# GpSimd's copies tied to points in VectorE's list, in a linear-attention kernel for one core

## Chip, cores, metric

One core of a Trainium2 chip. The time is device microseconds of one execution, the median over several; lower is better. The traced span of an execution is 1.8 us shorter than its time (kernel before: span 177.8, time 179.6), so spans are compared with spans and times with times. "Changed" is the kernel after the change. The engines' short names: PE is TensorE, DVE is VectorE, ACT is ScalarE, POOL is GpSimd, SP is SyncE (here it only issues the transfers). SBUF is the on-chip memory that all tiles but the matmul results are in; PSUM holds those. A run is called slow when it is over 1.5% above the fastest run of the same kernel in the same rounds, else fast.

## The reference, cut

```python
# B, H, S, D = 1, 32, 2048, 128, bf16
phi_q = jnp.where(q > 0, q + 1, jnp.exp(q)) + 1e-6
phi_k = jnp.where(k > 0, k + 1, jnp.exp(k)) + 1e-6
kv  = einsum("bhsd,bhse->bhde", phi_k, v)
z   = einsum("bhsd->bhd", phi_k)
num = einsum("bhqd,bhde->bhqe", phi_q, kv)
den = einsum("bhqd,bhd->bhq", phi_q, z)[..., None] + 1e-6
return num / den
```

The kernel uses phi(x) = (min(exp(x), 1) + eps) + max(x, 0) and keeps the two terms apart, as two matmuls into one PSUM tile. A head has 16 tiles of 128 rows.

## The kernel before, the parts concerned

Every piece of work has a name and stands in a fixed list for its engine; a list is run in order, and each piece waits for the pieces that it names.

```python
NI, NO, NE, NR, NV, NQ, NK = 7, 12, 2, 2, 2, 2, 2     # buffers: inputs, outputs, em, rk, v1, ...
WARM = (60, 30)                                        # dummy matmuls at the start, in batches
def kv_parts(h): return WHOLE
def gate(name, h): return []                           # no extra waits
# --- cut ---
# em: min(exp(k),1)+eps; all 16 tiles, in SBUF, DVE
add("DVE", f"em{h}.{i}", ... tensor_scalar(em_sb, em_sb, 1.0, EPS, op0=ALU.min, op1=ALU.add) ...)
# relu(k): tiles 0-7 on DVE, tiles 8-15 on GpSimd
add("DVE", f"rkd{h}.{i}", ... tensor_scalar(rk_sb, k_sb, 0.0, None, op0=ALU.max) ...)
add("POOL", f"rkp{h}.{i}", ... tensor_scalar(rk_sb, k_sb, BIG, 0.0, op0=ALU.min, op1=ALU.max),
    over("ldk", ...) + freed(NR, h, ("kv", kv_parts)) + gate("rkp", h))
# v beside its column of ones, on GpSimd
add("POOL", f"v1{h}.{i}", ... tensor_copy(v1_sb, v_sb) ...,
    [f"ldv{h}.{i}"] + freed(NV, h, ("kv", kv_parts)) + gate("v1", h))
# kv{h}: 32 matmuls; T{h}: 16 transposes of q; n{h}.0 / n{h}.1: 12 and 4 tiles of num and den
# r{h}.0: reciprocal of 12 den (PSUM); f{h}.0: num * that, 12 tiles (PSUM to SBUF); r.1, f.1: 4 tiles
# emq{h}: as em, for q; rqb{h}: relu of 8 transposed q tiles, read from PSUM
```

One steady stretch of the DVE list: `r9.1 rqb11 f9.1 r10.0 f10.0 emq11.0 em13.0 rkd13.0`. The SyncE list holds all loads and stores; it has `... st18.0 st25.0 ldv30.0 ldk31.0 ...` near its end.

## Time and profile before

| | before |
|---|---|
| median time | 177.51 us (177.2 to 177.63, 3 runs) |
| traced span | 177.8 us |
| busy: PE, DVE, ACT, POOL | 161.9, 158.4, 154.4, 71.5 us |
| DMA bytes | 67.12 MB |

The busy times are summed over the span. Three of the four are within 24 us of the span, and the transfers are busy for 95.1% of it, so the question is in which stretches, and for what, one engine waits for another. Two lines of the groups of instructions on GpSimd say when its work starts today. Columns: line, engine, operation, shape and count; busy us, mean ns; idle before it and what ended that.

```profile
L318 POOL TENSOR_SCALAR la<-la 128x1024 bf16<-128x1024 bf16 x32 | 36.1, 1137 | 44.1 <-PE la L329 33.5 <-DMA la<-in_k_dram 10.6
L322 POOL COPY la<-la 128x1024 int32<-128x1024 int32 (+1 forms) x33 | 35.3, 1076 | 44.0 <-PE la L329 22.4 <-DMA la<-in_v_dram 21.7
```

L329 is the kv product. GpSimd is idle until a kv product frees a buffer, or a load lands, and then starts at once: nothing relates its starts to DVE.

### The profile page before, as it was taken

To read this page: it belongs to the slowest core of one execution; us is meant where nothing else is said; L and a number is where in the kernel's file an instruction comes from. 1 tells how busy PE (TensorE), PEld (TensorE's weight loads), DVE (VectorE), ACT (ScalarE), POOL (GpSimd) and SP (SyncE) were. 2 spreads that over 40 slices of the span, in tenths; PEclk is the share of its full clock that TensorE was granted. 3 is DMA by queue.
4 is the path that set the end of the run, shared out by engine and by line. 5 is a ranking of instruction groups with operands and counts; after the bars stand their busy time and mean duration, and the time that the engine had idled before them with its cause. 6 is when DMAs were issued, how large, how long until landed. Compare 5 with 4: busy or idle time off the path is not lost.

```text
span 177.8 us, 6416 instructions
## 1 busy us (share of the span) xinstructions
PE 161.9 (91%) x2842; PEld 158.1 (89%) x2842; DVE 158.4 (89%) x266; ACT 154.4 (87%) x131; POOL 71.5 (40%) x71
## 2 busy tenths in 40 slices
PE   2986999999999999999889999988999989999870
PEld 1976999999999999999789999978999889989770
DVE  0156899999999999998999999999999999989973
ACT  2599799999999999999898999978999979994600
POOL 1253818417454246262723626264256424360000
PEclk9999999999999999999999999999999999999968
DMA  5999999999999999999999999999999945999973
GB/s 171 323 407 416 411 404 406 412 404 410 408 406 409 406 417 411 407 411 417 412 417 414 420 414 416 416 414 417 412 405 418 414 196 183 285 417 412 418 313 120
DMA packets 19179, 67.52 MB, mean 380 GB/s; under 512 B 2128, under 2 KB 2512, under 8 KB 19152
## 3 DMA queue, kind: packets, MB, share of 16 engines
q1 hardware_dynamic: 19152, 67.12, 95.1%
q8 instruction: 22, 0.36, 0.8%
q14 instruction: 5, 0.04, 0.1%
HBM read 50.33 MB, written 16.78 MB: 377 GB/s over the span
## 4 chain that ended last, share of the span: by engine, by line
PE 43%; DVE 20%; DMA 18%; issue 5%; SPq 4%; ACT 4%; POOL 3%; DVEq 0%; POOLq 0%
PE la L329 17%; DMA la<-in_k_dram 11%; PE la L364 9%; PE la L366 8%; PE la L340 8%; DVE la L380 8%; DMA out_dram<-la 7%; SPq L296 4%; DVE la L314 4%; DVE la L311 3%; DVE la L352 2%; ACT la L343 2%; DVE la L345 2%; POOL la L318 2%; POOL la L322 2%
## 5 line engine op out<-in xcount | busy, mean ns | idle before, releaser
L380 DVE TENSOR_TENSOR la<-la 128x1536 bf16<-128x1536 f32 (+2 forms) x65 | 77.7, 1199 | 2.0 <-DMA out_dram<-la 1.4
L366 PE MATMUL la<-la 128*128 128x129 bf16 x512 | 69.2, 222 | 0.0
L364 PE MATMUL la<-la 128*128 128x129 bf16 x512 | 69.1, 221 | 0.0
L329 PE MATMUL la<-la 128*128 128x129 bf16 x1024 | 64.0, 219 | 2.0 <-ACT la L349 1.4
L343 ACT ACTIVATE la<-la 128x2048 bf16<-128x2048 bf16 (+1 forms) x33 | 60.1, 1825 | 6.5 <-PE la L366 6.0
L308 ACT ACTIVATE la<-la 128x2048 bf16<-128x2048 bf16 (+1 forms) x33 | 61.3, 1860 | 2.1 <-DMA la<-in_k_dram 1.9
L329 PEld LDWEIGHTS la<-la 128*128 128x128 bf16 x1024 | 59.9, 97 | 2.7 <-DVE la L278 1.5
L318 POOL TENSOR_SCALAR la<-la 128x1024 bf16<-128x1024 bf16 x32 | 36.1, 1137 | 44.1 <-PE la L329 33.5
L322 POOL COPY la<-la 128x1024 int32<-128x1024 int32 (+1 forms) x33 | 35.3, 1076 | 44.0 <-PE la L329 22.4
L366 PEld LDWEIGHTS la<-la 128*128 128x128 bf16 x512 | 50.0, 98 | 0.0
L364 PEld LDWEIGHTS la<-la 128*128 128x128 bf16 x512 | 47.8, 98 | 0.0
L340 PE MATMUL la<-la 128*128 128x128 bf16 x512 | 34.8, 222 | 7.0 <-DMA la<-in_q_dram 3.6
L340 PEld LDWEIGHTS la<-la 128*128 128x128 bf16 x512 | 29.6, 99 | 9.0 <-issue 4.0
L359 PE MATMUL la<-la 128*128 128x3 bf16 (+1 forms) x192 | 32.6, 170 | 2.5 <-DVE la L380 2.5
L349 ACT ACTIVATE la<-la 128x1024 bf16<-128x1024 bf16 x32 | 32.6, 1019 | 2.5 <-PE la L340 2.5
L311 DVE TENSOR_SCALAR la<-la 128x2048 bf16<-128x2048 bf16 (+1 forms) x33 | 23.3, 706 | 3.1 <-ACT la L308 3.1
L314 DVE TENSOR_SCALAR la<-la 128x1024 bf16<-128x1024 bf16 x32 | 18.0, 566 | 7.4 <-DMA la<-in_k_dram 7.3
L345 DVE TENSOR_SCALAR la<-la 128x2048 bf16<-128x2048 bf16 (+1 forms) x33 | 22.3, 677 | 0.4 <-ACT la L343 0.4
L359 PEld LDWEIGHTS la<-la 128*128 128x128 bf16 x192 | 18.9, 99 | 3.5 <-DVE la L380 3.1
L352 DVE TENSOR_SCALAR la<-la 128x1024 bf16<-128x1024 bf16 x32 | 21.3, 667 | 0.7 <-ACT la L343 0.7
L373 DVE RECIPROCAL la<-la 128x12 f32<-128x12 f32 (+2 forms) x65 | 12.8, 198 | 2.2 <-PE la L366 1.4
L334 ACT ACTIVATE la<-la 128x129 bf16<-128x129 f32 x32 | 9.0, 281 | 1.0 <-PE la L329 1.0
(14 smaller groups left out, 13.5 us busy)
## 6 DMA issues: line engine op xcount, KB each, us to landing
la<-in_k_dram SPq DMA_DIRECT2D x31, 512.0 KB, 13.9
la<-in_q_dram SPq DMA_DIRECT2D x31, 512.0 KB, 13.9
la<-in_v_dram SPq DMA_DIRECT2D x31, 512.0 KB, 13.3
out_dram<-la SPq DMA_DIRECT2D x31, 512.0 KB, 13.2
la<-in_q_dram SPq DMA_DIRECT2D x2, 256.0 KB, 3.0
la<-in_k_dram SPq DMA_DIRECT2D x2, 256.0 KB, 5.2
la<-in_v_dram SPq DMA_DIRECT2D x2, 256.0 KB, 7.6
out_dram<-la SPq DMA_DIRECT2D x2, 192.0 KB, 2.1
```

The source lines that it names most:

```text
L308: add("ACT", f"ek{h}.{i}", lambda e, a=a, b=b: e.activation(em_sb[:, h % NE, a:b], k_sb[:, h % NI, a:b], ACT.Exp), [f"ldk{h}.{i}"] + freed ...
L311: add("DVE", f"em{h}.{i}", lambda e, a=a, b=b: e.tensor_scalar(em_sb[:, h % NE, a:b], em_sb[:, h % NE, a:b], 1.0, EPS, op0=ALU.min, op1=AL ...
L318: add("POOL", f"rkp{h}.{i}", lambda e, a=a, b=b: e.tensor_scalar(rk_sb[:, h % NR, a:b], k_sb[:, h % NI, a:b], BIG, 0.0, op0=ALU.min, op1=A ...
L322: add("POOL", f"v1{h}.{i}", lambda e, a=a, b=b: e.tensor_copy(v1_sb[:, h % NV, a:b, 0:D].bitcast(i32), v_sb[:, h % NI, a:b].bitcast(i32)), ...
L329: ins = e.matmul(kv_ps, lhsT=src[:, j], rhs=v1_sb[:, h % NV, j, 0:NC], start=(j + part == 0), stop=(j == NT - 1 and part == 1))
L340: ins = e.transpose(xT[:, j], q_sb[:, h % NI, j], ident[:])
L343: add("ACT", f"eq{h}.{i}", lambda e, a=a, b=b: e.activation(emq_sb[:, h % NQ, a:b], xT[:, a:b], ACT.Exp), [f"T{h}.{i}"] + freed(NQ, h, ("n ...
L349: add("ACT", f"rqa{h}", lambda e: e.activation(rq_sb[:, h % NQ, 0:n], xT[:, 0:n], ACT.Relu), over("T", h, q_parts, 0, n) + freed(NQ, h, (" ...
L359: e.matmul(_ap(o_ps[:, :], o + D, [[NC, m]]), lhsT=ones[:], rhs=epsr[:, 0:m], start=True, stop=False, skip_group_check=True)
L364: e.matmul(to, lhsT=emq_sb[:, h % NQ, t], rhs=kvs_sb[:, h % NK], start=False, stop=False, skip_group_check=True)
L366: ins = e.matmul(to, lhsT=rq_sb[:, h % NQ, t], rhs=kvs_sb[:, h % NK], start=False, stop=True, skip_group_check=True)
L380: return e.tensor_tensor(out=_ap(o_sb[:, :, :, :], first(o_sb[:, h % NO, t0, 0:1]) - first(o_sb[:, :, :, :]), [[m * D, nb], [D, m], [1, D] ...
```

## The change

The intent: put GpSimd's two pieces of a head beside DVE work that doesn't need the SBUF ports which the two engines share (the prediction names the page and the trace lines for this), and order everything else around that. The diff, cut to its core:

```diff
-WARM = (60, 30)
+WARM = (60, 15, 15)
 def kv_parts(h):
-    return WHOLE
+    return HALVES
 def gate(name, h):
-    return []
+    if h < 3:
+        return []
+    return [f"r{h - 3}.0"] if name == "v1" else [f"f{h - 3}.0"]
 # the five lists are written anew; two excerpts:
 # DVE, around head 10
-  r9.1 rqb11 f9.1 r10.0 f10.0 emq11.0 em13.0 rkd13.0 r10.1 rqb12 f10.1
+  r9.1 rqb11 f9.1 emq11.0 r10.0 rkd13.0 f10.0 em13.0 rqb12 r10.1 f10.1
 # SP, the end
-  ldk30.0 st17.0 ldv29.0 ldq29.0 st18.0 st25.0 ldv30.0 ldk31.0 st16.0 ldv31.0 st21.0 ldq31.0 st23.0 ...
+  ldv29.0 ldq29.0 ldq30.0 st15.0 ldv30.0 ldv31.0 ldk31.0 ldq31.0 st16.0 st17.0 st18.0 ...
```

More of the change, by code (lines that the diff above doesn't have):

```diff
@@ L54, in gate @@
 def gate(name, h):
-    return []
+    if h < 3:
+        return []
+    return [f"r{h - 3}.0"] if name == "v1" else [f"f{h - 3}.0"]
 ORDER = {
     "PE": """
-        T0.0 T0.1 w1 w0 T1.0 kv0.0 kv1.0 n0.0 n0.1 T2.0 kv2.0 n1.0 T3.0 n1.1 kv3.0 n2.0 T4.0 n2.1 kv4.0 n3.0 T5.0
-        n3.1 kv5.0 n4.0 T6.0 n4.1 kv6.0 n5.0 n5.1 T7.0 kv7.0 n6.0 T8.0 n6.1 kv8.0 n7.0 T9.0 n7.1 kv9.0 n8.0 T10.0
-        n8.1 kv10.0 n9.0 T11.0 n9.1 kv11.0 n10.0 T12.0 n10.1 kv12.0 n11.0 T13.0 n11.1 kv13.0 n12.0 T14.0 n12.1
-        kv14.0 n13.0 T15.0 n13.1 kv15.0 n14.0 T16.0 n14.1 kv16.0 n15.0 T17.0 n15.1 kv17.0 n16.0 n16.1 T18.0 kv18.0
-        n17.0 T19.0 n17.1 kv19.0 n18.0 T20.0 n18.1 kv20.0 n19.0 T21.0 n19.1 kv21.0 n20.0 T22.0 n20.1 kv22.0 n21.0
-        T23.0 n21.1 kv23.0 n22.0 T24.0 n22.1 kv24.0 n23.0 n23.1 T25.0 kv25.0 n24.0 T26.0 n24.1 kv26.0 n25.0 T27.0
-        n25.1 kv27.0 n26.0 T28.0 n26.1 kv28.0 n27.0 T29.0 n27.1 kv29.0 n28.0 T30.0 n28.1 kv30.0 n29.0 T31.0 n29.1
-        kv31.0 n30.0 n30.1 n31.1 n31.0 n31.2
+        w2 T0.1 T0.0 w1 w0 T1.0 kv0.0 kv0.1 n0.0 kv1.0 kv1.1 T2.0 n0.1 n1.0 kv2.0 kv2.1 T3.0 n1.1 kv3.0 kv3.1 n2.0
+        T4.0 n2.1 kv4.0 kv4.1 n3.0 T5.0 n3.1 kv5.0 kv5.1 n4.0 T6.0 n4.1 kv6.0 kv6.1 n5.0 T7.0 n5.1 kv7.0 kv7.1 n6.0
+        T8.0 n6.1 kv8.0 kv8.1 n7.0 T9.0 n7.1 kv9.0 kv9.1 n8.0 T10.0 n8.1 kv10.0 kv10.1 n9.0 T11.0 n9.1 kv11.0 kv11.1
+        n10.0 T12.0 n10.1 kv12.0 kv12.1 n11.0 T13.0 n11.1 kv13.0 kv13.1 n12.0 T14.0 n12.1 kv14.0 kv14.1 n13.0 T15.0
+        n13.1 kv15.0 kv15.1 n14.0 T16.0 n14.1 kv16.0 kv16.1 n15.0 T17.0 n15.1 kv17.0 kv17.1 n16.0 T18.0 n16.1 kv18.0
+        kv18.1 n17.0 T19.0 n17.1 kv19.0 kv19.1 n18.0 T20.0 n18.1 kv20.0 kv20.1 n19.0 T21.0 n19.1 kv21.0 kv21.1 n20.0
+        T22.0 n20.1 kv22.0 kv22.1 n21.0 T23.0 n21.1 kv23.0 kv23.1 n22.0 T24.0 n22.1 kv24.0 kv24.1 n23.0 T25.0 n23.1
+        kv25.0 kv25.1 n24.0 T26.0 n24.1 kv26.0 kv26.1 n25.0 T27.0 n25.1 kv27.0 kv27.1 n26.0 T28.0 n26.1 kv28.0
+        kv28.1 n27.0 T29.0 n27.1 kv29.0 kv29.1 n28.0 T30.0 n28.1 kv30.0 kv30.1 n29.0 T31.0 n29.1 kv31.0 kv31.1 n30.0
+        n30.1 n31.0 n31.1 n31.2
@@ L68 @@
     """,
     "DVE": """
-        v1ones0 rkd0.0 em0.1 rkd1.0 rqb0 em0.0 eps0 em1.0 emq0.1 emq0.0 rqb1 v1ones1 eps1 rkd2.0 eps2 ones emq1.0
-        rkd3.0 em2.0 r0.0 f0.0 em3.0 rqb2 r0.1 rkd4.0 f0.1 r1.0 emq2.0 f1.0 em4.0 rkd5.0 r1.1 rqb3 f1.1 r2.0 f2.0
-        emq3.0 em5.0 rkd6.0 rqb4 r2.1 f2.1 r3.0 emq4.0 f3.0 em6.0 r3.1 rqb5 rkd7.0 f3.1 r4.0 emq5.0 f4.0 em7.0 r4.1
-        f4.1 rqb6 r5.0 f5.0 emq6.0 rkd8.0 em8.0 r5.1 rqb7 f5.1 r6.0 emq7.0 f6.0 rkd9.0 em9.0 r6.1 rqb8 f6.1 r7.0
-        emq8.0 f7.0 rkd10.0 em10.0 r7.1 rqb9 f7.1 r8.0 emq9.0 f8.0 rkd11.0 em11.0 r8.1 rqb10 f8.1 r9.0 rkd12.0 f9.0
@@ L75 @@
-        emq10.0 em12.0 r9.1 rqb11 f9.1 r10.0 f10.0 emq11.0 em13.0 rkd13.0 r10.1 rqb12 f10.1 rkd14.0 r11.0 emq12.0
-        f11.0 em14.0 r11.1 rqb13 f11.1 r12.0 f12.0 emq13.0 rkd15.0 em15.0 r12.1 rqb14 f12.1 rkd16.0 r13.0 emq14.0
-        f13.0 em16.0 r13.1 rqb15 f13.1 r14.0 f14.0 emq15.0 em17.0 rkd17.0 r14.1 rqb16 f14.1 r15.0 rkd18.0 f15.0
-        emq16.0 em18.0 r15.1 f15.1 rqb17 r16.0 f16.0 emq17.0 em19.0 rkd19.0 r16.1 rqb18 f16.1 r17.0 emq18.0 f17.0
-        rkd20.0 em20.0 r17.1 rqb19 f17.1 r18.0 f18.0 emq19.0 rkd21.0 em21.0 r18.1 rqb20 f18.1 r19.0 emq20.0 f19.0
@@ L80 @@
-        em22.0 rkd23.0 rkd22.0 rqb21 r19.1 r20.0 f19.1 f20.0 emq21.0 em23.0 rkd24.0 rqb22 r20.1 f20.1 r21.0 emq22.0
-        f21.0 em24.0 rqb23 r21.1 f21.1 r22.0 emq23.0 rkd25.0 f22.0 em25.0 r22.1 f22.1 rqb24 r23.0 f23.0 emq24.0
-        rkd26.0 em26.0 r23.1 rqb25 f23.1 r24.0 emq25.0 f24.0 em27.0 rkd27.0 r24.1 rqb26 f24.1 r25.0 emq26.0 f25.0
-        rkd28.0 em28.0 r25.1 rqb27 f25.1 r26.0 emq27.0 f26.0 rkd29.0 em29.0 r26.1 rqb28 f26.1 r27.0 emq28.0 f27.0
-        rkd30.0 em30.0 r27.1 rqb29 f27.1 r28.0 f28.0 emq29.0 rkd31.0 em31.0 rqb30 r28.1 f28.1 r29.0 emq30.0 f29.0
@@ L85 @@
-        emq31.0 r29.1 rqb31 r30.0 f29.1 f30.0 r30.1 f30.1 r31.1 f31.1 r31.0 r31.2 f31.0 f31.2
+        rkd0.0 ones v1ones0 emq0.1 rqb0 emq0.0 rkd1.0 em0.0 em0.1 v1ones1 eps0 eps1 em1.0 eps2 emq1.0 rqb1 r0.0 f0.0
+        rkd3.0 rkd2.0 em2.0 em3.0 rqb2 emq2.0 r0.1 f0.1 r1.0 rkd4.0 f1.0 em4.0 rqb3 r1.1 rkd5.0 f1.1 r2.0 emq3.0
+        f2.0 em5.0 rqb4 r2.1 rkd6.0 f2.1 r3.0 emq4.0 f3.0 em6.0 rqb5 r3.1 rkd7.0 f3.1 r4.0 emq5.0 f4.0 em7.0 rqb6
+        r4.1 f4.1 r5.0 emq6.0 f5.0 em8.0 rqb7 r5.1 f5.1 rkd8.0 r6.0 emq7.0 f6.0 em9.0 rqb8 r6.1 f6.1 rkd10.0 rkd9.0
@@ new lines @@
+        r7.0 emq8.0 f7.0 rkd11.0 rqb9 r7.1 em10.0 f7.1 r8.0 emq9.0 f8.0 em11.0 rqb10 r8.1 f8.1 rkd12.0 r9.0 emq10.0
+        f9.0 em12.0 r9.1 rqb11 f9.1 emq11.0 r10.0 rkd13.0 f10.0 em13.0 rqb12 r10.1 f10.1 rkd14.0 r11.0 emq12.0 f11.0
+        em14.0 r11.1 rqb13 f11.1 rkd15.0 r12.0 emq13.0 f12.0 em15.0 r12.1 rqb14 f12.1 rkd16.0 r13.0 emq14.0 f13.0
+        em16.0 r13.1 rqb15 f13.1 rkd17.0 r14.0 emq15.0 f14.0 em17.0 r14.1 rqb16 f14.1 rkd18.0 r15.0 emq16.0 f15.0
+        em18.0 rqb17 r15.1 rkd19.0 f15.1 r16.0 emq17.0 f16.0 em19.0 rqb18 r16.1 rkd20.0 f16.1 r17.0 emq18.0 f17.0
@@ new lines @@
+        em20.0 rqb19 r17.1 rkd21.0 f17.1 r18.0 emq19.0 f18.0 em21.0 rqb20 r18.1 f18.1 rkd22.0 r19.0 emq20.0 f19.0
+        em22.0 rqb21 r19.1 f19.1 rkd23.0 r20.0 emq21.0 f20.0 em23.0 rqb22 r20.1 rkd24.0 f20.1 r21.0 emq22.0 f21.0
+        em24.0 r21.1 rqb23 f21.1 emq23.0 r22.0 rkd25.0 f22.0 em25.0 rqb24 r22.1 f22.1 rkd26.0 emq24.0 r23.0 f23.0
+        em26.0 r23.1 rqb25 f23.1 emq25.0 r24.0 rkd27.0 f24.0 em27.0 rqb26 r24.1 f24.1 emq26.0 r25.0 f25.0 em28.0
+        rqb27 r25.1 f25.1 rkd29.0 r26.0 rkd28.0 f26.0 emq27.0 rqb28 em29.0 r26.1 f26.1 r27.0 rkd30.0 f27.0 emq28.0
@@ L86 @@
+        rqb29 r27.1 emq29.0 f27.1 r28.0 em30.0 f28.0 em31.0 rqb30 r28.1 f28.1 r29.0 rkd31.0 f29.0 emq30.0 emq31.0
+        rqb31 r29.1 r30.0 f29.1 f30.0 r30.1 f30.1 r31.0 f31.0 r31.1 f31.1 r31.2 f31.2
     """,
     "ACT": """
-        rqa0 ek0.1 ek0.0 eq0.1 eq0.0 ek1.0 eq1.0 kvs0 rqa1 ek2.0 kvs1 ek3.0 eq2.0 kvs2 rqa2 ek4.0 eq3.0 kvs3 rqa3
+        eq0.1 eq0.0 rqa0 ek0.0 ek1.0 ek0.1 eq1.0 kvs0 rqa1 ek2.0 kvs1 ek3.0 eq2.0 rqa2 kvs2 ek4.0 eq3.0 kvs3 rqa3
         ek5.0 eq4.0 kvs4 rqa4 ek6.0 eq5.0 kvs5 rqa5 ek7.0 eq6.0 kvs6 rqa6 ek8.0 eq7.0 kvs7 rqa7 ek9.0 eq8.0 kvs8
@@ L92 @@
         ek18.0 eq17.0 kvs17 rqa17 ek19.0 eq18.0 kvs18 rqa18 ek20.0 eq19.0 kvs19 rqa19 ek21.0 eq20.0 kvs20 rqa20
-        ek22.0 eq21.0 rqa21 kvs21 ek23.0 eq22.0 kvs22 rqa22 ek24.0 eq23.0 kvs23 rqa23 ek25.0 eq24.0 kvs24 rqa24
-        ek26.0 eq25.0 kvs25 rqa25 ek27.0 eq26.0 kvs26 rqa26 ek28.0 eq27.0 kvs27 rqa27 ek29.0 eq28.0 kvs28 rqa28
-        ek30.0 eq29.0 kvs29 rqa29 ek31.0 eq30.0 kvs30 rqa30 eq31.0 kvs31 rqa31
+        ek22.0 eq21.0 kvs21 rqa21 ek23.0 eq22.0 kvs22 rqa22 ek24.0 eq23.0 kvs23 rqa23 ek25.0 eq24.0 kvs24 rqa24
@@ L96 @@
+        ek26.0 eq25.0 kvs25 rqa25 ek27.0 eq26.0 kvs26 rqa26 ek28.0 eq27.0 kvs27 rqa27 ek29.0 eq28.0 rqa28 kvs28
+        ek30.0 eq29.0 kvs29 rqa29 ek31.0 eq30.0 kvs30 rqa30 eq31.0 rqa31 kvs31
     """,
     "POOL": """
-        ident0 ident rkp0.0 rkp1.0 v10.1 v10.0 v11.0 v12.0 rkp2.0 rkp3.0 v13.0 v14.0 rkp5.0 rkp4.0 v15.0 rkp6.0
-        v16.0 v17.0 v18.0 rkp7.0 rkp8.0 rkp9.0 v19.0 rkp10.0 v110.0 rkp11.0 v111.0 v112.0 rkp13.0 rkp12.0 v113.0
-        v114.0 rkp15.0 rkp14.0 v115.0 rkp16.0 v117.0 v116.0 rkp17.0 rkp18.0 v119.0 v118.0 rkp19.0 rkp20.0 v121.0
@@ L101 @@
-        v120.0 rkp21.0 v122.0 rkp23.0 rkp22.0 v123.0 rkp24.0 v124.0 v125.0 v126.0 rkp25.0 rkp26.0 rkp27.0 v127.0
-        rkp28.0 v128.0 rkp29.0 v129.0 rkp30.0 rkp31.0 v130.0 v131.0
+        ident0 ident rkp0.0 v10.0 v10.1 v11.0 rkp1.0 rkp2.0 v12.0 rkp3.0 v13.0 v14.0 rkp4.0 v15.0 rkp5.0 v16.0
+        rkp6.0 v17.0 rkp7.0 v18.0 rkp8.0 v19.0 rkp9.0 v110.0 rkp10.0 v111.0 rkp11.0 v112.0 rkp12.0 v113.0 rkp13.0
+        v114.0 rkp14.0 v115.0 rkp15.0 v116.0 rkp16.0 v117.0 rkp17.0 v118.0 rkp18.0 v119.0 rkp19.0 v120.0 rkp20.0
@@ L103 @@
+        v121.0 rkp21.0 v122.0 rkp22.0 v123.0 rkp23.0 v124.0 rkp24.0 v125.0 rkp25.0 v126.0 rkp26.0 v127.0 rkp27.0
+        v128.0 rkp28.0 v129.0 rkp29.0 v130.0 rkp30.0 v131.0 rkp31.0
     """,
     "SP": """
-        ldq0.0 ldq0.1 ldk0.0 ldk0.1 ldk1.0 ldq1.0 ldv0.1 ldv0.0 ldv1.0 ldk2.0 ldv2.0 ldk3.0 ldq2.0 ldv3.0 ldq3.0
-        ldk4.0 ldq8.0 ldv4.0 ldk5.0 ldq4.0 ldv5.0 ldk6.0 ldk7.0 ldq5.0 ldv6.0 ldq6.0 ldv8.0 ldk8.0 ldv7.0 ldq7.0
-        ldk9.0 ldq9.0 ldk11.0 ldq12.0 ldq11.0 ldv9.0 ldk10.0 ldq10.0 ldk14.0 ldv10.0 ldq13.0 ldk15.0 ldk12.0 ldv11.0
@@ L108 @@
-        ldk13.0 ldv13.0 ldv12.0 ldv15.0 ldv14.0 st0.0 ldq14.0 ldq17.0 ldq16.0 ldv16.0 ldq15.0 ldq18.0 ldk16.0
-        ldq19.0 ldv20.0 ldv17.0 ldk18.0 st1.0 st2.0 ldk17.0 st4.0 ldk19.0 ldv19.0 ldv18.0 st3.0 ldv21.0 ldv22.0
-        st5.0 st6.0 st10.0 ldk20.0 ldk22.0 ldv23.0 ldq20.0 ldk21.0 ldq21.0 st9.0 ldk23.0 st7.0 ldq22.0 st8.0 ldq23.0
-        ldk24.0 ldv25.0 ldq26.0 ldq27.0 ldk25.0 ldv24.0 ldk26.0 ldq24.0 st11.0 ldk27.0 ldv26.0 ldq28.0 ldq25.0
-        st14.0 ldq30.0 st12.0 ldv27.0 ldk28.0 st13.0 ldk29.0 ldv28.0 st15.0 ldk30.0 st17.0 ldv29.0 ldq29.0 st18.0
@@ L113 @@
-        st25.0 ldv30.0 ldk31.0 st16.0 ldv31.0 st21.0 ldq31.0 st23.0 st20.0 st24.0 st27.0 st26.0 st28.0 st19.0 st22.0
-        st29.0 st30.0 st31.1 st31.0 st31.2
+        ldq0.0 ldq0.1 ldk0.0 ldk0.1 ldk1.0 ldq1.0 ldv0.0 ldv0.1 ldv1.0 ldk2.0 ldq2.0 ldk3.0 ldv2.0 ldq3.0 ldk4.0
+        ldv3.0 ldv4.0 ldq4.0 ldk5.0 ldv5.0 ldv6.0 ldq5.0 ldk6.0 ldk7.0 ldv7.0 ldk8.0 ldq6.0 ldk9.0 ldv8.0 ldq7.0
+        ldq8.0 st0.0 ldk10.0 ldq9.0 st1.0 ldv9.0 ldv10.0 ldv11.0 ldq10.0 ldk11.0 ldk12.0 ldk13.0 ldv12.0 ldv13.0
@@ new lines @@
+        ldq11.0 st2.0 ldq12.0 st3.0 ldq13.0 ldq14.0 ldk14.0 ldv14.0 ldk15.0 ldv15.0 st4.0 ldk16.0 ldq15.0 ldk17.0
+        ldq16.0 ldv16.0 ldv17.0 ldv18.0 ldk18.0 ldq17.0 ldk19.0 ldq18.0 st5.0 ldv19.0 ldk20.0 ldk21.0 ldq19.0
+        ldq20.0 ldv20.0 ldv21.0 ldv22.0 ldv23.0 ldk22.0 st6.0 st7.0 st8.0 ldk23.0 ldq21.0 ldk24.0 ldq22.0 ldk25.0
+        ldv24.0 ldk26.0 ldq23.0 ldq24.0 ldk27.0 st9.0 ldv25.0 st10.0 ldq25.0 ldv26.0 st11.0 ldq26.0 ldv27.0 st12.0
+        ldk28.0 ldk29.0 ldq27.0 st13.0 ldv28.0 st14.0 ldk30.0 ldq28.0 ldv29.0 ldq29.0 ldq30.0 st15.0 ldv30.0 ldv31.0
@@ L115 @@
+        ldk31.0 ldq31.0 st16.0 st17.0 st18.0 st19.0 st20.0 st21.0 st22.0 st23.0 st24.0 st25.0 st26.0 st27.0 st28.0
+        st29.0 st30.0 st31.0 st31.1 st31.2
     """,
```

## The prediction

> **What bounds the kernel now.** I read the busy shares first. Four engines and the DMA lie within eight points of each other, so no share alone names the bound:
>
> ```profile
> PE 161.9 (91%) x2842; PEld 158.1 (89%) x2842; DVE 158.4 (89%) x266; ACT 154.4 (87%) x131; POOL 71.5 (40%) x71
> DMA  5999999999999999999999999999999945999973
> q1 hardware_dynamic: 19152, 67.12, 95.1%
> ```
>
> Next the busy time by stretch. Columns: window, its length, busy us of PE, PEld, DVE, ACT, POOL, then clock, DMA share, GB/s.
>
> ```profile
> 31.00:80.00 49.00, 49.00 (x892) 48.77 (x890) 48.16 (x83) 49.00 (x41) 21.76 (x21) 1.00 1.03 409
> 80.00:99.00 19.00, 17.57 (x314) 16.92 (x312) 18.04 (x30) 17.41 (x16) 8.70 (x8) 1.00 1.03 416
> 113.00:129.00 16.00, 14.58 (x263) 14.22 (x261) 15.83 (x26) 14.41 (x13) 6.77 (x6) 1.00 1.03 413
> 141.00:156.00 15.00, 14.21 (x256) 13.87 (x254) 15.00 (x25) 14.01 (x12) 5.77 (x5) 1.00 0.70 244
> ```
>
> From 31 to 80 us PE and ACT never rest; that is the floor of the steady state. The kv products of heads 4 to 15 (T and kv starts, read off the timeline) start every 4.73 us: 30.58 for head 4, 82.70 for head 15, 52.1/11. In 80:99, 113:129 and 141:156 PE and ACT rest together for 1.4, 1.4 and 0.8 us while DVE is nearly full: there DVE sets the pace. The sum from kv4 (30.58) to kv31 (163.97) is 133.4 us; 27 heads at 4.73 are 127.7. So **5.7 us of stalls** lie between them.
>
> What makes DVE late is in its lines and its timeline:
>
> ```profile
> L314 DVE TENSOR_SCALAR la<-la x32: 356/419/1275, 6.7 to 160.9; 128x1024 bf16<-128x1024 bf16 x32
> L345 DVE TENSOR_SCALAR la<-la x33: 423/630/1104, 13.7 to 166.1; 128x2048 bf16<-128x2048 bf16 x31, 128x1024 bf16<-128x1024 bf16 x2
> L352 DVE TENSOR_SCALAR la<-la x32: 653/660/692, 10.4 to 166.8; 128x1024 bf16<-128x1024 bf16 x32
> 120.88 1.27 DVE L314 TENSOR_SCALAR la<-la 128x1024 bf16<-128x1024 bf16 x1
> 120.84 1.04 POOL L318 TENSOR_SCALAR la<-la 128x1024 bf16<-128x1024 bf16 x1 [2.27 <-PE la L329]
> 83.57 1.76 DVE L380 TENSOR_TENSOR la<-la 128x1536 bf16<-128x1536 f32 x1 [0.86 <-DMA out_dram<-la]
> ```
>
> The reader is to see min/median/max. DVE's half of relu(k) (L314) takes 0.42 us or, six times, 1.07 to 1.28: each of those lies beside a GpSimd instruction, as at 120.84, and lasts until that one is through. The DVE relu that reads PSUM (L352) is beside GpSimd 25 times and never leaves 653 to 692 ns.
>
> Last the DMA queue's own timeline:
>
> ```profile
> 132.63 15.72 SPq L388 DMA_DIRECT2D out_dram<-la  x2
> 148.40 0.43 SPq L296 DMA_DIRECT2D la<-in_v_dram  x1
> ```
>
> SyncE stands 15 us in front of st25, which its list puts ahead of the last loads; the queue runs dry. In 140:155 the DMA moved 338, 130 and 265 GB/s in thirds of 5 us instead of 415: 2.56 MB, or **6.2 us of transfer time**, lost.
>
> **What the Trainium skill says.** "SBUF — State Buffer", section "Who interferes with whom": DVE in a 2-port mode and GpSimd take the shared ports as an exclusive lock, whoever issues first, and the other fully blocks. The trace agrees: 0.42 us becomes 1.26, that is +0.84 against a GpSimd instruction of 1.04. "VectorE: DVE Perf Modes", section "Mode 2×_2P — use both read ports for one tensor": tensor_scalar from SBUF may use it, PSUM sources may not. The trace agrees: L352 (PSUM) stays at 660 ns and the 12-tile product at 1739 to 1759 ns beside GpSimd or not. "DMA: Bandwidth & Descriptors", section "Where 436 GB/s comes from", lets the HBM side bind at about 358 GB/s; this trace holds 409 to 416, which decides.
>
> **The change part by part.** No arithmetic changes: the same 2842 matmuls, the same DVE, ACT and POOL work (DVE sheds no tile; the lists differ only in order). Five things move.
>
> 1. *The gates.* GpSimd's v copy of head h waits for the 12-tile reciprocal r(h-3).0, its relu(k) for the product f(h-3).0. Today both run as soon as kv(h-2) is done, wherever DVE happens to be. On DVE, r.0 is followed back to back by emq ([...]0.63 us), which takes the ports first; the copy then runs inside f.0, which lasts 1.75 us and reads PSUM. After f.0 comes em (0.68), which again is first; relu(k) then has rqb and r.1 to run in, start to start 0.60 + 0.1 to 0.2. The gates themselves cost PE nothing. With n(h).0 ending at 0, r.0 is at 0.15, so the copy is done at about 1.9 and relu(k) at 0.84+1.75+0.6+1.04 = 4.2, for a kv that starts at 1.6+4.73 = 6.3.
>
> 2. *What the old collisions cost.* From kv4 on: relu(k) four times 0.84 (at 90.7, 115.4, 120.9, 140.9) = 3.4; em at 85.2, 0.43; emq at 137.6, 148.0, 159.9, 3 x 0.44 = 1.3. Sum 5.1 us of DVE time. The stores' waits add 1.4 us (f13 waits 0.86 for st1, f28 0.53 for st16, buffers not written out). 6.5 us of DVE gave the 5.7 us of PE.
>
> 3. *What collisions stay.* relu(k) on GpSimd takes 1.04 us, and rqb with r.1 cover only about 0.7. Where the new list puts DVE's relu next (heads f1, f2, f3, f15, f16, f17, f20) or an em (f7, f26, f27), that one waits about 0.45 us. Ten times 0.45 = 4.5 us of DVE, but in small pieces. DVE's undisturbed cycle, by start-to-start spacings, is em 0.60 + rqb 0.60 + r.1 0.09 + rkd 0.33 + f.1 0.60 + r.0 0.14 + emq 0.55 + f.0 1.66 = 4.57, or 4.69 with rkd elsewhere, against PE's 4.73; and n(h+1).0 starts about 0.8 us after f(h).0 ends. One such piece is absorbed; three in a row (0.3 each over the period) run out. I put **0.8 us** on PE for all.
>
> 4. *The start.* kv in halves lets PE begin on tiles 0 to 7 before em and v of 8 to 15 are there. But kv2 waits for v2, now the tenth 512 KB transfer. Landings in the trace come every 1.28 us and the ninth is at 18.4, so v2 lands at 19.7, its copy is done at 20.8, and kv2 stays at 21. After that the two early collisions on DVE (em2 1.52 us, relu 1.07) are gone and kv4 can start near 30.0 instead of 30.6. Gain **0.6 us**.
>
> 5. *The SP list.* Stores stand where they are ready, and the last load (q31) is slot 111 of 128 with st16 to st31 behind it. I counted slots against a landing of 7.0 + 1.27 x slot. Tight places: k6 32.4 against a need at 33.1; q6 37.5 against 38.1; st9 117.5 against f21 at 119.4. No entry waits for something later than about 8 us before its turn, so I expect no dry queue. DMA then ends at 177.8 - 6.2 (the hole) - 3.4 (in 170:177 the trace moved 1.48 MB, worth 3.6 of 7 us) = 168.2: below compute.
>
> Sum on the compute side: kv4 at 30.0, 27 x 4.73 = 127.7 gives kv31 at 157.7; +0.8 is 158.5; the tail from kv31 to the end was 13.8 and I take 13.8, of which a DVE free of backlog (0.7 late at f29.0) could save half a microsecond or more. **172.3 us**, down 5.2, of 177.51.
>
> **The rivals.**
> *DVE stays the bound.* If the ten remaining collisions cost 0.85 rather than 0.45 (GpSimd getting the lock ahead of em or emq because the gate's event comes first), DVE loses 8 us, more than today, and the time is 176 to 178. For it: DVE is 98% busy even in 31:80. Against: emq starts 0.14 us after r.0 starts, before r.0's recorded end, so a semaphore cannot be ahead of it.
> *The transfers become the bound.* A store that SyncE meets before its product is written would stop the loads behind it, as st25 does now; k6 and q6 have 0.7 us in hand. Some 2 us of stall: 174 to 175. Against: the 16 last stores are behind every load.
> *The hole is all there was.* Were DMA the only bound, taking out its 6.2 us would give 171.6 whatever GpSimd does. Against: kv30 waits only 0.5 us in connection with it, and f28 0.53.
> *The clean case.* No stall and a shorter tail: 157.7 + 12.9 = 170.6.
>
> **Range and chances.** The low end is the clean case, 170.6; the high end lets half of the first rival or the whole of the second come true, 175.0. The 2% line is 173.96, 1.7 us above my sum, and most of what I subtract is read directly off the trace. Faster 0.80, within 0.18, slower 0.02.
>
> **What would show each step.** Right: L314's maximum falls from 1.27 us to under 0.9, with the stretched ones beside GpSimd's relu only; L345 has none over 0.7; GpSimd's copies grow from a mean of 1.10 to about 1.5 us, since they now stand in front of emq, costing nobody; no DMA slice under 400 GB/s between 10 and 165 us; PE at 9 in every slice of the steady state; kv31 near 158.5. Wrong: a median L314 or L311 over 0.8 us; a PE wait of several us on the GpSimd lines; a queue wait of over 5 us on L388 ahead of a load; a period above 4.75 with PE and ACT idle together.

## The result, and the profile after

The changed kernel took **172.99 us** (172.7 to 173.15, 4 runs) beside 177.35 for the kernel before (the three runs of above and a fourth). A ratio here is the mean time of one kernel's fast runs over that of the other's of the same rounds, so not quite the ratio of the medians: 0.9755, 95% interval 0.9727 to 0.9782.

The changed kernel's page, rows of busy time, DMA share and GB/s in 40 slices:

```profile
PE 160.8 (94%) x2842; PEld 158.5 (93%) x2842; DVE 154.1 (90%) x266; ACT 153.3 (90%) x131; POOL 85.6 (50%) x71
DMA  4999999999999999999999999999999999999874
GB/s 152 366 409 412 413 405 406 410 407 416 412 416 404 411 415 411 416 411 404 416 411 411 411 411 418 409 409 418 415 416 414 416 418 416 411 421 411 348 297 175
```

No slice between the first two and the last three is under 404 GB/s: the hole is gone. DVE is busy 4.3 us less for the same 266 instructions; GpSimd shows 14 us more. The same stretches as in the prediction (columns as there):

```profile
31.00:80.00 49.00, 48.96 (x888) 48.51 (x886) 47.99 (x82) 48.75 (x43) 27.93 (x21) 1.00 1.03 412
80.00:99.00 19.00, 19.00 (x350) 18.97 (x348) 18.73 (x34) 19.00 (x18) 11.24 (x9) 1.00 1.02 411
113.00:129.00 16.00, 16.00 (x296) 15.97 (x293) 15.76 (x30) 16.00 (x15) 9.08 (x7) 1.00 1.03 415
141.00:156.00 15.00, 14.86 (x269) 14.50 (x267) 14.48 (x25) 14.69 (x14) 8.19 (x7) 1.00 1.03 416
```

In the second and third, where PE and ACT rested 1.4 us each before, both are now busy throughout, and DVE is the one with time to spare; in the fourth PE rests 0.1 us instead of 0.8. The lines of DVE's relu(k), of emq and of GpSimd's copy and relu(k), min/median/max in ns:

```profile
L318 DVE TENSOR_SCALAR la<-la x32: 360/416/1260, 5.8 to 157.6; 128x1024 bf16<-128x1024 bf16 x32
L349 DVE TENSOR_SCALAR la<-la x33: 409/629/837, 7.0 to 160.7; 128x2048 bf16<-128x2048 bf16 x31, 128x1024 bf16<-128x1024 bf16 x2
L326 POOL COPY la<-la x33: 616/1371/1376, 10.0 to 153.2; 128x1024 int32<-128x1024 int32 x31, 128x512 int32<-128x512 int32 x2
L322 POOL TENSOR_SCALAR la<-la x32: 1041/1412/1537, 6.5 to 155.5; 128x1024 bf16<-128x1024 bf16 x32
```

GpSimd's instructions are now the ones that stand in line: 1.37 and 1.41 us at the median against 1.04 undisturbed. Only one DVE relu is still over 1 us, that of head 2 at 19.2 us, and the gate does not prevent it: two DVE relus stand in a row after f0.0 there, and GpSimd's relu of head 3, let go by f0.0, comes between them (19.08 to 20.23). How one head looks, in the timeline of DVE (emq, 12-tile product, em, 4-tile reciprocal, rqb, 4-tile product, relu; three lines left out). A timeline line has start and length in us, engine, line, operation and shape; in brackets is the idle time before it, with what ended that:

```profile
81.90 0.63 DVE L349 TENSOR_SCALAR la<-la 128x2048 bf16<-128x2048 bf16 x1
82.45 1.74 DVE L384 TENSOR_TENSOR la<-la 128x1536 bf16<-128x1536 f32 x1
84.11 0.68 DVE L315 TENSOR_SCALAR la<-la 128x2048 bf16<-128x2048 bf16 x1
...
86.15 0.42 DVE L318 TENSOR_SCALAR la<-la 128x1024 bf16<-128x1024 bf16 x1
```

and of GpSimd:

```profile
82.05 1.37 POOL L326 COPY la<-la 128x1024 int32<-128x1024 int32 x1 [1.09 <-DVE la L377]
84.28 1.41 POOL L322 TENSOR_SCALAR la<-la 128x1024 bf16<-128x1024 bf16 x1 [0.86 <-DVE la L384]
```

A GpSimd record begins here at the release, so I take the time above the undisturbed 1.04 us as its wait for the ports. The copy is let go 0.15 us after emq has begun, waits 0.33 us, runs 1.04 us under the product that reads PSUM and is through at 83.42. The relu is let go 0.17 us after em has begun, waits 0.37 us and is through at 85.69, before DVE's relu at 86.15.

Where the traced spans differ, 177.8 to 171.2: to the start of kv4, 0.5 us (30.58, now 30.09); from kv4 to kv31, 133.4 to 128.5, **4.9 us**; from kv31 to the end, 13.8 to 12.6.

### The profile page after: what moved, and what is told of

Its sections match the earlier page's. It is cut to its first block, busy times and chain, and to the rows that moved or that the text cites.

```text
span 171.2 us, 6462 instructions
## 1 busy us (share of the span) xinstructions
PE 160.8 (94%) x2842; PEld 158.5 (93%) x2842; DVE 154.1 (90%) x266; ACT 153.3 (90%) x131; POOL 85.6 (50%) x71
## 4 chain that ended last, share of the span: by engine, by line
ACT 55%; PE 32%; DVE 8%; DMA 2%; issue 1%; SPq 0%; DVEq 0%
ACT la L347 23%; ACT la L312 20%; PE la L333 10%; ACT la L353 10%; PE la L344 6%; PE la L368 6%; PE la L370 6%; DVE la L384 4%; PE la L291 3%; ACT la L338 3%; DMA la<-in_q_dram 2%; DVE la L356 1%; DVE la L349 1%; PE la L363 1%; DVE la L377 1%
## 5 line engine op out<-in xcount | busy, mean ns | idle before, releaser
L370 PE MATMUL la<-la 128*128 128x129 bf16 x512 | 68.0, 220 | 0.0
L368 PE MATMUL la<-la 128*128 128x129 bf16 x512 | 68.0, 219 | 0.0
L333 PE MATMUL la<-la 128*128 128x129 bf16 x1024 | 64.0, 219 | 0.0
L326 POOL COPY la<-la 128x1024 int32<-128x1024 int32 (+1 forms) x33 | 40.5, 1228 | 40.8 <-DVE la L377 34.7
L322 POOL TENSOR_SCALAR la<-la 128x1024 bf16<-128x1024 bf16 x32 | 44.4, 1387 | 29.7 <-DVE la L384 23.8
L315 DVE TENSOR_SCALAR la<-la 128x2048 bf16<-128x2048 bf16 (+1 forms) x33 | 22.9, 697 | 3.0 <-ACT la L312 3.0
L356 DVE TENSOR_SCALAR la<-la 128x1024 bf16<-128x1024 bf16 x32 | 21.8, 680 | 2.1 <-ACT la L347 1.5
L349 DVE TENSOR_SCALAR la<-la 128x2048 bf16<-128x2048 bf16 (+1 forms) x33 | 21.3, 647 | 1.2 <-ACT la L347 1.2
L318 DVE TENSOR_SCALAR la<-la 128x1024 bf16<-128x1024 bf16 x32 | 14.2, 448 | 5.8 <-DMA la<-in_k_dram 5.8
L377 DVE RECIPROCAL la<-la 128x12 f32<-128x12 f32 (+2 forms) x65 | 12.8, 198 | 1.6 <-PE la L370 0.9
```

What stands on the lines that cost most here:

```text
L322: add("POOL", f"rkp{h}.{i}", lambda e, a=a, b=b: e.tensor_scalar(rk_sb[:, h % NR, a:b], k_sb[:, h % NI, a:b], BIG, 0.0, op0=ALU.min, op1=A ...
L326: add("POOL", f"v1{h}.{i}", lambda e, a=a, b=b: e.tensor_copy(v1_sb[:, h % NV, a:b, 0:D].bitcast(i32), v_sb[:, h % NI, a:b].bitcast(i32)), ...
L333: ins = e.matmul(kv_ps, lhsT=src[:, j], rhs=v1_sb[:, h % NV, j, 0:NC], start=(j + part == 0), stop=(j == NT - 1 and part == 1))
L356: add("DVE", f"rqb{h}", lambda e: e.tensor_scalar(rq_sb[:, h % NQ, n:], xT[:, n:], 0.0, None, op0=ALU.max), over("eq", h, q_parts, n, NT) ...
L368: e.matmul(to, lhsT=emq_sb[:, h % NQ, t], rhs=kvs_sb[:, h % NK], start=False, stop=False, skip_group_check=True)
L370: ins = e.matmul(to, lhsT=rq_sb[:, h % NQ, t], rhs=kvs_sb[:, h % NK], start=False, stop=True, skip_group_check=True)
```

## Experiments

Two figures from each trace go with the times. *Surplus*: over DVE's relu(k), em and emq that begin after 30 us and last at least 15% beyond 0.42, 0.68 and 0.63 us, their lengths when undisturbed, the sum of what is beyond. *kv4 to kv31*: between the starts of those two products; 27 heads at 4.725 us (kv15 to kv25 of the changed kernel, 47.25/10) would be 127.6. The medians take in slow runs, three of 12 of the kernel before with the new list and two of 7 of the kernel before, again; of the fast ones alone they are 178.34 and 177.63.

| run | median us | ratio to before (95%) | surplus us | kv4 to kv31 us |
|---|---|---|---|---|
| before | 177.51 | | 5.2 | 133.4 |
| before, again | 178.91 | 1.0008 (0.9949 to 1.0066) | 5.3 | 133.0 |
| changed | 172.99 | 0.9755 (0.9727 to 0.9782) | 0.7 | 128.5 |
| changed, again | 172.89 | 0.9774 (0.9722 to 0.9825) | 0.7 | 128.5 |
| before + new transfer list | 178.39 | 1.0024 (0.9979 to 1.0069) | 5.7 | 132.2 |
| changed, old transfer list | 174.63 | 0.9812 (0.9741 to 0.9882) | 0.8 | 128.6 |
| changed, no gates | 185.20 | 1.0412 (1.0324 to 1.0500) | 14.4 | 140.0 |
| changed, gate on copy only | 174.87 | 0.9845 (0.9783 to 0.9907) | 5.1 | 129.9 |
| changed, gate on relu only | 181.14 | 1.0225 (1.0156 to 1.0293) | 11.3 | 136.4 |
| before + gates | 192.21 | 1.0851 (1.0785 to 1.0917) | 18.5 | 143.9 |
| changed, kv whole | 173.97 | 0.9775 (0.9709 to 0.9841) | 1.4 | 129.0 |
| changed, 30 warming matmuls | 172.57 | 0.9733 (0.9688 to 0.9778) | 0.7 | 128.5 |
| the same, start reordered | 173.35 | 0.9802 (0.9742 to 0.9862) | 0.7 | 128.5 |

The surplus less what kv4 to kv31 is above 127.6, over the number of stretched instructions, is alike in the five variants with many of them: 1.1 us over 10 (new transfer list), 2.0 over 33 (no gates), 2.8 over 27 (copy only), 2.5 over 33 (relu only), 2.2 over 22 (before + gates). So, as an estimate from these traces, some 0.06 to 0.11 us of each stretch is absorbed and the rest is paid. It also shows at single places: in the kernel before kv21 to kv23 take 11.17 us, 1.7 more than two undisturbed periods, and the DVE relus of heads 22 and 24 that fall there are 1.69 us too long; in the changed kernel the same stretch takes 9.45.

Theory: the gain is DVE time no longer lost to GpSimd at the shared ports. Rival: it is the hole in the transfers, closed by the new SyncE list.

**The transfer list alone, put into the kernel before.**

```diff
 "SP": """
-    ... ldq29.0 st18.0 st25.0 ldv30.0 ldk31.0 st16.0 ...      (the whole list of before)
+    ... ldq30.0 st15.0 ldv30.0 ldv31.0 ldk31.0 ldq31.0 st16.0 ...   (the whole list of changed)
```

> The kernel before with only the new SyncE list (transfers) of the changed kernel; engine lists and gates as before. Theory: the compute lists with their port collisions set the end and the 6.2 us hole in the transfers is beside the critical path, so only the 1.4 us of DVE waits for stored buffers and about 0.5 us of waiting at kv30 go: 175.5 to 177.3 us, with the six long L314 (1.07 to 1.28 us) still there and no hole in the DMA row. Rival (the hole was all there was): 171.5 to 173.5 us.

178.39 us, ratio 1.0024: nothing gained, a little over what I expected. The DMA row of its page, then (next fence) two of its stretches:

```profile
DMA  5999999999999999999999999999999999997354
```

```profile
113.00:129.00 16.00, 14.58 (x264) 14.22 (x262) 15.83 (x26) 14.41 (x13) 6.76 (x6) 1.00 1.03 416
164.00:168.00 4.00, 3.03 (x54) 2.68 (x51) 3.34 (x7) 2.12 (x3) 0.00 (x0) 1.00 0.12 42
```

The hole before the end is gone; instead the transfers run out of work at 164 to 168 us, at 42 GB/s, waiting for products. And in 113:129 PE rests 1.4 us exactly as before. The rival falls: 6.2 us of transfer time were given back and were not on the path. DVE's 1.4 us of waits for stored buffers are gone as expected, and kv4 to kv31 is 1.2 us shorter than in the first trace of the kernel before, 0.8 than in the second; five DVE relus are long, where I expected the same six.

**The changed kernel with the old transfer list.** The reverse edit.

> The changed kernel with only the old SyncE list put back. Theory: engines keep their quiet DVE; st25 is ready about 5 us earlier than before, so the hole shrinks to 1 to 2 us, the wait of f13 for its store buffer comes back: 173 to 174.5 us. Rival (the transfer list was all there was): 176.5 to 177.5 us.

174.63 us, near what the theory had (174.5 at most, missed by a tenth). SyncE again stands before st25, from 131.8 for 12.3 us instead of 15.7, in its queue's timeline:

```profile
131.76 12.32 SPq L392 DMA_DIRECT2D out_dram<-la  x2
```

From 140 to 155 us the transfers average 353 GB/s; against 415 that is 2.2 us lost, not 1 to 2, and the wait of f13 for its store buffer did not come back. Yet kv4 to kv31 is 128.6 us. In this trace the old list costs 0.8 us at the start (kv4 at 30.85 instead of 30.09, and 29.53 in the changed kernel's second trace) and 0.3 us at the end; against the changed kernel's own ratios, 0.9755 and 0.9774, its interval leaves open whether that is more than noise.

**No gates.**

```diff
-    return [f"r{h - 3}.0"] if name == "v1" else [f"f{h - 3}.0"]
+    return []
```

> The changed kernel with no gates: GpSimd's v copy and relu(k) start as soon as their buffers are free. Theory: the copies now begin at the end of kv(h-2), wherever DVE is, relu(k) of DVE, em and emq collide again with 0.4 to 0.84 us each; at 5 us or more of lost DVE time past 30 us the time is 175 to 177.5 us. Rival (the new order alone keeps the ports apart, or collisions cost nothing): 172.7 to 173.3 us.

185.2 us, 12 us above the changed kernel: the direction of the theory, far beyond the size that I gave. The new order without the gates is worse than the old one. DVE at one em, and GpSimd beside it:

```profile
79.72 1.55 DVE L313 TENSOR_SCALAR la<-la 128x2048 bf16<-128x2048 bf16 x1
```

```profile
79.69 1.04 POOL L324 COPY la<-la 128x1024 int32<-128x1024 int32 x1 [2.51 <-PE la L331]
```

The copy, let go by the end of a kv product, is 0.03 us ahead of em, and em takes 1.55 instead of 0.68 us. Past 30 us ten ems, fourteen relus and nine emqs are stretched: surplus 14.4 us, and kv4 to kv31 12.4 us above 127.6.

**The gates alone, in the kernel before** (with the GpSimd list of the changed kernel, in which each head's copy and relu come in turn; the old one swaps some pairs and would wait on later heads).

```diff
 def gate(name, h):
-    return []
+    if h < 3:
+        return []
+    return [f"r{h - 3}.0"] if name == "v1" else [f"f{h - 3}.0"]
 "POOL": """ (the changed kernel's list) """
```

> The kernel before with the two gates and the GpSimd order that they need, everything else as before. Theory (the gates fix a place in the DVE list, and are only as good as the instructions that stand there): about 20 of the old list's heads have two [...]DVE operations right after the 12-tile product (emq then em, or relu then em), so relu(k) on GpSimd takes the ports between the two and the second waits up to 0.85 us; that is up to 17 us of DVE time, of which the slack of 0.17 us a head takes some 4: 183 to 190 us, slower than before. Rival (the gates alone are the gain): 172 to 174.5 us.

192.2 us, 2 us beyond the range and 14.8 us slower than before. DVE after a 12-tile product, and GpSimd:

```profile
86.30 0.68 DVE L347 TENSOR_SCALAR la<-la 128x2048 bf16<-128x2048 bf16 x1
86.90 1.26 DVE L316 TENSOR_SCALAR la<-la 128x1024 bf16<-128x1024 bf16 x1
```

```profile
86.47 1.41 POOL L320 TENSOR_SCALAR la<-la 128x1024 bf16<-128x1024 bf16 x1 [0.78 <-DVE la L382]
```

emq is first, GpSimd's relu waits from 86.47, and when the ports come free it has them, not DVE's next instruction: the relu at 86.90 takes 1.26 us. The old list has two such DVE operations in a row after most products; 22 instructions are stretched past 30 us. So the gates are no gain in themselves. Gates and the new order belong together; either half alone costs 8 to 15 us over the kernel before. Within the new order, DVE's list was not tried apart from those of PE and ACT, so that DVE's is the one the gates need rests on the timelines above.

**One gate at a time.**

```diff
-    return [f"r{h - 3}.0"] if name == "v1" else [f"f{h - 3}.0"]
+    return [f"r{h - 3}.0"] if name == "v1" else []          # copy only
+    return [] if name == "v1" else [f"f{h - 3}.0"]          # the other run: relu only
```

> The changed kernel with the gate on the v copy kept and that on relu(k) taken off. Theory: relu(k) follows the copy at once on GpSimd, starts about 1.8 us after the 12-tile reciprocal and is in the way of em, which comes when the product ends: about 0.5 us a head, DVE's cycle 5.1 us against 4.73: 179 to 184 us, the long ones being em. Rival (one gate is enough, since GpSimd's order carries the other along): 172.7 to 174 us.

174.87 us: here neither theory nor rival was met. GpSimd's relu follows the copy at 83.88 and is through at 84.92:

```profile
84.60 0.86 DVE L315 TENSOR_SCALAR la<-la 128x2048 bf16<-128x2048 bf16 x1
```

em began at 84.60, so 0.32 us were in GpSimd's hands, but em lasted only 0.18 us longer. The place of the collision was right and its size was a third of the 0.5 us assumed. em is stretched in 24 heads, and with three other instructions the surplus is 5.1 us, about as much as in the kernel before. It costs 2.3 us over 127.6 where that one lost 5.8, its store waits of 1.4 included. The kernel before with the new transfer list had no such waits: there 5.7 us of surplus in ten mostly larger pieces cost 4.6. If about 0.1 us of each piece is absorbed, that is over half of a piece of 0.18 us and an eighth of one of 0.84.

> The changed kernel with the gate on relu(k) kept and that on the v copy taken off. Theory: the copy of the next head starts right behind relu(k) of this one, near the end of the 4-tile product, where DVE's relu(k) or emq stands: 0.25 to 0.75 us a head, 177 to 183 us, the long ones being L318 and emq. Rival (one gate is enough): 172.7 to 174 us.

181.14 us, as expected. The copy starts right behind GpSimd's relu, and DVE's relu takes the blow; DVE, then GpSimd:

```profile
83.62 0.97 DVE L318 TENSOR_SCALAR la<-la 128x1024 bf16<-128x1024 bf16 x1
```

```profile
83.28 1.03 POOL L326 COPY la<-la 128x1024 int32<-128x1024 int32 x1
```

The gate on the copy, with the other in place, is thus worth 8 us in this order. The gate on relu(k) is worth about 2: 1.4 us of it is in kv4 to kv31; the interval of the ratio, 0.9783 to 0.9907, is just clear of one of the changed kernel's and overlaps the other.

**kv in one piece.**

```diff
 def kv_parts(h):
-    return HALVES
+    return WHOLE
 # and kv0.1 ... kv31.1 struck from PE's list
```

> The changed kernel with the kv products in one piece of 16 tiles again (the second halves struck from PE's list). Theory: relu(k) on GpSimd is done about 2 us before kv starts, so the halves matter only at the start: kv0 0.3 to 0.8 us later, in all 173.0 to 173.7 us. Rival (halves give GpSimd the slack that the gates take): a period above 4.75 us and over 175 us.

173.97 us, 0.3 above the range, with an interval that overlaps the changed kernel's. The start behaves as said: kv0 and kv4 are 0.3 us later (kv4 at 30.35). Another 0.5 us is lost in kv4 to kv31, with one DVE relu of 1.20 us at 56.1 that the changed kernel doesn't have, which I had not foreseen. The period elsewhere is 4.73 us: the halves are not what lets GpSimd be late.

**Trying for more.** In the changed kernel 75 of the dummy matmuls stand between T0 and T1.

```diff
-WARM = (60, 15, 15)
+WARM = (30, 15, 15)
```

> The changed kernel with 30 instead of 60 warming matmuls in the last of the three batches. Theory: in the changed kernel's trace 75 of them stand in front of T1 from 6.5 to 11.95 us although its q landed at 9.3; eq1 on ScalarE could start at 12.4 instead of 13.0, and from kv1 on PE and ACT run without a gap, so everything moves 0.6 us forward: 172.2 to 172.6 us. Rival (TensorE's clock has then not risen, or the start is hidden by the loads): 173 us or more, with a lower clock in the first slices.

172.57 us. kv4 starts at 29.22 instead of 30.09, in line with the theory, but kv4 of the changed kernel's second trace is at 29.53, and the intervals 0.9688 to 0.9778 and 0.9722 to 0.9825 overlap. Not shown to be faster. The mean granted clock was 0.995, the changed kernel's 0.996. On top of it:

```diff
-    ... rqb1 r0.0 f0.0 rkd3.0 rkd2.0 em2.0 em3.0 ...
+    ... rqb1 rkd2.0 r0.0 f0.0 em2.0 rkd3.0 em3.0 ...
```

> The changed kernel with 30 warming matmuls in the last batch and, on DVE, relu(k) of head 2 ahead of the first reciprocal and em2 ahead of relu(k) of head 3. Theory: with 30 alone kv2 waited 0.32 us for em2, which stood behind two relus of 1.11 and 1.25 us; that wait and the collisions before em2 go, kv2 about 0.3 to 0.5 us earlier than 20.65: 172.0 to 172.5 us, 0.5 to 1.0 us under the changed kernel run beside it. Rival (the loads or PE's own list hold kv2 to kv4 anyway): within 0.3 us of 172.6.

> The changed kernel as it is, once more in the same rounds as the trial of the start, to compare the two on one chip: 172.7 to 173.3 us again, the spread of its runs well below the kernel before's 3 us.

173.35 and 172.89 us: no gain; the first is above both what the theory and what the rival had, the second is as expected. The two early collisions did go (em2 at 18.0 instead of 20.4 us), and kv2 started at 20.58, against 20.65 in the run with 30 alone. First landings differ by up to 1.5 us from trace to trace (GpSimd's first relu starts at 6.5 in the changed kernel's trace and at 8.0 in this one), so I put the start down to the loads, which is not tested. The changed kernel stays the best that is shown.

**The kernel before, traced again.**

> The kernel before, unchanged, for a second trace of it. Its first trace is of an execution that took 179.6 us, 2 us over the median, so part of what was read there may be that execution's own. Theory (the collisions depend on when transfers land, as nothing ties GpSimd to DVE): the long relu, em and emq instructions stand at other heads, their sum past 30 us differs by 1 us or more from the first trace's 5.2, and the span by 1 to 3 us. Rival (the collisions are a fixed property of the lists): the same heads, the same sum within 0.3 us.

Here the rival was right. The same eight instructions after 30 us are long (relu of heads 17, 22, 24, 27; em16; emq of 25, 27, 29), surplus 5.3 us: with given lists the collisions recur. The transfers still have a say: with the new transfer list alone five of the eight recur and five others come. Its lines of relu(k) and emq:

```profile
L314 DVE TENSOR_SCALAR la<-la x32: 357/418/1283, 5.4 to 159.1; 128x1024 bf16<-128x1024 bf16 x32
L345 DVE TENSOR_SCALAR la<-la x33: 410/631/1262, 12.4 to 164.3; 128x2048 bf16<-128x2048 bf16 x31, 128x1024 bf16<-128x1024 bf16 x2
```

The span was 174.7 instead of 177.8 us: 1.3 us earlier at kv4, 0.4 between, 1.4 less in the tail. Start and tail vary from run to run; the 133.0 against 128.5 us in the middle, 4.5 us, is the gain that stays, and it is close to the difference of the medians, 4.4.

## Why the prediction was right, step by step

- *DVE's collisions with GpSimd set the pace*: right. kv4 to kv31 grows with the surplus across the runs, from 0.7 to 18.5 us, once about 0.1 us a piece is taken off, while closing the hole in the transfers alone gained nothing.
- *The gates put the copy under f.0 and relu(k) behind em, at no cost to PE*: right, in the timeline above. The prediction's argument uses the new order (emq behind r.0, em behind f.0) but doesn't say that the gates do harm without it; the run with the gates alone shows it.
- *What the old collisions cost, 5.1 us*: 5.2 by the rule above, 5.3 in the second trace. Three small readings were off: 52.1/11 is 4.74 and not 4.73; the four engines within eight points count TensorE twice, as matmul and weight load; the DVE relu from PSUM is beside GpSimd 24 times, not 25.
- *What stays, ten times 0.45 us*: wrong in size. Five of the ten places were hit (relu of heads 19, 20, 21, 24; em10), and each costs 0.13 to 0.16 us, in all 0.7. Two terms were mis-sized. The step took em to hold the ports for its whole recorded time; GpSimd's relu had them 0.54 us after em's start, so that it overlaps DVE's relu of head 19 by 0.29 us (94.85 to 95.14) and not by 0.45. And it took the whole overlap as lost; that relu lasted only 0.15 us longer. The 0.8 us of PE stalls came out near (128.5 less 127.6 is 0.9), but by luck: 0.35 us of it is at head 10, where em is long, and about 0.45 at heads 28 to 30, where no instruction is long; what holds PE there stays open.
- *The start, 30.0 for kv4*: 30.09 and 29.53, but the gain of 0.6 us is not shown: the kernel before had kv4 at 30.58 and, in its second trace, at 29.26. The two early collisions did go (em2 0.68, relu of head 3 0.41 us), but others came (em1 1.33, relu of head 2 1.26), and kv2 was at 21.47 instead of 21. kv31 was put at 158.5 and came at 158.59 and 158.03.
- *The SP list, no dry queue*: right. The end of the transfers at 168.2, below compute, was not: the last store's packets ended at 170.0, after DVE's last work at 168.6.
- *The tail, 13.8 us*: 12.6 and 12.8. The kernel before had 12.5 in its second trace; the first, of an execution 2.1 us over the median, was longer than is usual. My sum of 172.3 was a span, so it is 171.2 that answers to it: 1.1 too high, by the tail's 1.2. The median of 172.99 lies nearer to the sum only because a time is 1.9 us more than a span, which is luck.
- *Signs*: L318 under 0.9 us holds past 30 us (0.57 at most) but not at the start (1.26). No emq over 0.7 us holds past 30 us (0.694) but not at 6.95 us (0.84). DMA at 400 GB/s and more up to 165 us holds up to 158 us only; then, with nothing but stores left, a slice has 348. GpSimd's copies were to be at 1.5 us and are at 1.37, again since the ports come free sooner.

## What to carry to other kernels

Where two engines share something that only one can hold, look at the maximum beside the median of each line, and count the surplus by place: here a fixed small part of each piece (about 0.1 us) was absorbed and the rest paid, so large pieces cost nearly their whole length. A wait that holds back the engine with time to spare can be worth microseconds, if it points at a spot in the busy engine's list where one short holder is followed by work that doesn't need the thing; order and wait have to be made together. A hole in the transfers is no proof that they bound the kernel: see first what they would have brought, and to whom.

## What the Trainium skill lacked or had wrong

- "SBUF — State Buffer", "Who interferes with whom": it has the lock held for the whole instruction, and does not say how that relates to the recorded times. Here GpSimd had the ports 0.48 us after the start of an emq recorded as 0.63 us, and 0.54 after that of an em recorded as 0.68, if it ran its undisturbed 1.04 us from then on: about 0.14 us before the recorded end. In the same way a blocked DVE instruction lost about 0.14 us less than its overlap: 0.18 of 0.32 us (em, gate on copy only), 0.55 of 0.69 (relu, gate on relu only), 0.87 of 1.01 (em, no gates). Whether the lock is let go early or the record runs on past it, the runs don't tell.
- The same section says that issue order decides who blocks. The runs add what happens with a third: a GpSimd instruction that is already waiting goes ahead of DVE's next one (relu at 86.90 us, 1.26 instead of 0.42, behind an emq that had been first).
- "DMA: Bandwidth & Descriptors", "Where 436 GB/s comes from": it lets the HBM side, about 358 GB/s, bind transfers between HBM and SBUF; loads and stores together held 404 to 421 GB/s here over most of the span. The page's section "Measured (HBM→SBUF, 128 partitions, SWDGE, issued from GpSimd)" says that 358 is each core's share when both cores of an HBM domain stream; this program runs on one core. So the figure is not refuted; the sentence lacks that condition.
- No page says how a DVE instruction's surplus turns into time: here 5.1 us in 27 pieces, most of 0.18, cost 2.3 us, and 14.4 us in 33 pieces, most of it in large ones, cost 12.4.
